# A linear-attention and Fourier-filter kernel: the transform split into even and odd bins, with a new instruction order

## The chip, the cores and the metric

One core of one Trainium2 chip. The metric is device time in microseconds of one execution; less is better. Engines: PE (TensorE, products; PEld its weight loads), DVE (VectorE), ACT (ScalarE), POOL (GpSimd, here only DMA issue and index tables), SP (SyncE, here only DMA issue).

## The reference

Shapes: q, k, v [8, 8, 576, 64], omega [128, 64], w_proj [512, 1536], filter_fft [576, 512], w_out [512, 512], all float32; the output is [8, 576, 512] float32.

```python
def phi(x):                                   # x: q or k, scaled by 64 ** -0.25
    proj = np.einsum('bhsd,md->bhsm', x, omega)
    h = proj - np.sum(x * x, axis=-1, keepdims=True) / 2.0
    h = h - np.max(h, axis=-1, keepdims=True)
    return np.exp(h) / np.sqrt(m)
kv = np.einsum('bhsm,bhsd->bhmd', k_p, v)
num = np.einsum('bhsm,bhmd->bhsd', q_p, kv)
den = np.einsum('bhsm,bhm->bhs', q_p, np.sum(k_p, axis=2))[..., None] + 1e-06
x = (num / den)                               # heads side by side: [8, 576, 512]
...
x1, x2, x3 = np.split(x @ w_proj, 3, axis=-1)
x2_conv = np.fft.irfft(np.fft.rfft(x2, n=S, axis=1) * np.fft.rfft(filter_fft, n=S, axis=0)[None], n=S, axis=1)
out = (x1 * x2_conv * x3) @ w_out
```

## The kernel before

**Two stages per batch.** `attention()` makes the rows of x, transposed to [512 columns, rows], in `xt`; `hyena()` does the projections, the circular convolution along the 576 rows and the output product. Each batch has 512 main rows (four tiles of 128) and 64 left rows; the left rows of two batches (a pair i) share one tile of 128, so that a pair is finished together (`xtl`, "left out").

**The transform.** 576 = 3 x 192. Rows are read as three chunks of 192. `fold` subtracts the third chunk from the first two (slots 0 and 1 of `xf`, 128 rows of each chunk, main rows alone) and adds all three (slot 3); `fold_rest` does the same for the last 64 rows of each chunk, which need the left rows (slot 2, both chunks side by side, and `xfl`). `project2` multiplies each slot by the middle third of w_proj, so that folding comes before the projection; the result is `x2`, slots 0 to 3, and `x2l`. `forward` then makes four banks of 128 spectral rows per batch: m = 0, 1, 2 of three products each (tables `fwb`, slots 2, 0, 1), for the bins that are no multiple of 3, and m = 3 of two products (`fwa`, `fwar`), for bins that are; one more bank, `xr`, for both batches of the pair (`fwn`, `fwnr`). ACT copies each bank to SBUF: m = 0 and 1 into `xs`, whose two banks are real and imaginary parts of the same bins, m = 2 and 3 into `sp`, where real and imaginary parts are the two partition halves of one bank. For those, two DMAs on SP's queue make `sw`, the copy with the halves exchanged. `spectrum` multiplies by the filter's spectrum on DVE: `ha`, `hb` for `xs`, `hps`, `hqs` for `sp` and `sw`. The inverse takes two column blocks at a time (g): three banks `pa`, even and odd of four products of 192 or 193 columns each, then ACT copies and DVE additions into `y`, and a multiplication by the gates `x13` (x1 times x3) gives `yt`. The output product with `wout` follows, per tile of 128 rows, an ACT copy and a DMA on SP.

**Tables and filter at the start.** `make_residues` scales index tables on ACT and reduces them on DVE; `sines` makes the sine and cosine tables `gtab`, `gta`, `gns` on ACT; `tables` turns them by PE transposes into `fwb`, `fwa`, `fwar`, `fwn`, `fwnr`. The filter is loaded in seven DMAs (`load_filter`), folded on DVE, transformed by the same tables, and moved into `hps` and `hqs` by DMAs on SP, as `split_out` has it: two ACT copies and four or five DMAs for a bank.

**The order.** Every operation is recorded by `Plan` and numbered; consecutive products into one bank are one number. `ORDER` is a list of these numbers, written out by hand or by a program beforehand, and `issue` emits them in that order (line 230, so that nearly all instructions of the profile have this line). Each engine runs its own instructions in this order, and a tile's buffer is given to the next tile of the same name when its last reader is done. PSUM has four banks named `h` and two double banks named `a`.

Lines of note: `turn_runs` (738 to 750) turns x for batches 0 and 1 by products with the identity into a float32 bank. `xs`, `sp`, `sw` and `bt` have two buffers each; `y` uses `bt` too. The last output tile, batch 7 tile 3, is copied half by DVE and half by ACT from one bank (1340 to 1354).

Of the kernel before, what the change touches and what calls it, by code (L numbers as in the profile page):

```python
# [26 lines left out]
599 29 33 31 34 56 30 9 0 32 57 3 5 4 38 27 39 28 6 2 40 35 50 49 7 51 52 45 46 55 53 11 12 23 47 41  # L27
42 43 71 99 24 48 72 138 8 85 97 44 70 1 26 54 74 73 16 18 13 86 25 87 10 88 37 76 586 64 98 588 589
36 65 100 67 69 58 66 68 600 89 59 90 91 590 75 60 62 61 143 149 92 63 140 93 112 114 150 152 154
155 587 145 14 22 21 111 591 113 151 153 161 101 108 110 156 94 102 107 109 103 104 105 157 163 162  # L30
159 95 106 164 139 158 160 165 96 115 116 126 127 211 120 181 121 128 182 123 229 122 124 125 117 20
144 172 223 118 119 174 175 177 166 230 167 176 135 178 133 593 224 171 247 134 136 131 129 225 173
130 132 227 596 168 169 170 17 19 214 595 603 602 604 179 180 615 617 248 195 196 197 616 146 618
192 193 194 147 231 233 15 78 611 613 249 213 189 217 623 597 250 592 598 190 186 191 625 594 187
188 258 260 624 83 221 286 626 200 201 202 204 203 137 183 185 184 226 321 612 198 205 206 609 199
734 614 228 207 601 661 322 208 610 232 673 662 262 660 81 212 235 236 80 289 670 736 209 290 234
632 251 264 735 257 605 210 259 148 215 77 218 606 674 671 252 667 216 672 237 291 295 668 296 238
293 675 607 292 253 261 347 627 142 737 254 350 676 628 141 255 669 256 294 679 680 284 222 738 687
663 82 348 220 79 263 298 297 740 664 608 665 299 688 629 300 726 677 678 728 239 240 241 242 244
630 243 245 246 265 266 631 666 305 685 686 641 642 643 267 275 633 648 649 650 689 647 652 655 651  # L40
645 276 277 693 694 705 278 691 692 706 634 636 635 656 657 707 653 708 644 709 637 279 306 280 281
282 654 639 646 268 269 307 308 309 270 681 658 659 323 682 310 283 324 365 325 271 366 272 219 303
739 359 304 367 369 371 372 360 319 301 320 741 695 362 342 619 273 690 727 302 700 696 343 697 364
621 373 344 274 823 361 822 729 374 722 723 363 316 724 480 311 620 730 699 701 318 474 725 313 745
315 312 732 747 710 684 683 349 622 345 638 640 702 698 703 746 375 731 749 748 317 314 704 346 713
714 758 326 355 329 742 733 330 743 353 288 287 351 331 760 893 840 895 368 385 370 824 744 386 829
841 711 712 337 451 452 327 376 377 378 328 720 338 750 842 751 719 752 334 335 379 830 285 332 383
384 333 425 476 354 897 848 899 849 356 357 894 755 339 336 394 756 432 757 477 358 434 340 715 896
753 825 387 721 754 905 716 341 832 844 845 388 717 826 827 907 419 481 396 828 428 781 782 783 759
898 900 718 430 762 393 862 833 389 863 856 857 771 917 761 773 390 395 919 831 391 768 769 784 838  # L50
770 839 786 772 427 397 84 843 774 763 775 764 765 767 776 766 381 846 399 847 429 785 834 835 777
778 852 853 431 398 433 836 850 837 851 400 392 380 483 352 787 382 800 801 401 402 788 435 789 790
794 403 404 906 405 908 486 882 411 436 876 489 412 795 877 858 859 491 802 437 438 413 791 780 921
878 879 860 855 864 865 861 406 493 922 803 495 779 439 854 881 407 793 408 440 883 804 414 415 866
416 818 918 488 479 424 923 819 490 475 924 453 454 417 920 870 867 869 871 455 418 874 884 909 911
426 880 891 890 449 820 805 409 821 796 872 450 446 410 469 797 496 448 798 925 868 497 873 470 471
927 885 792 926 928 932 886 892 441 498 443 934 499 887 472 799 910 912 806 888 945 423 422 875 807
947 492 473 442 444 1027 500 501 502 1092 901 903 1094 946 445 485 889 1009 447 902 948 949 904 503
1093 958 494 462 960 959 463 1095 459 942 943 482 961 944 929 930 1014 962 460 950 951 952 464 1015
537 808 1084 1086 931 815 933 465 816 809 810 811 817 1080 1082 505 954 953 466 467 935 484 420 421  # L60
478 936 461 1081 456 457 1012 1013 955 971 973 956 458 507 937 1083 938 468 543 544 957 963 939 545
1010 1011 940 1035 546 1036 913 812 1085 563 915 564 1087 540 539 972 914 984 1028 941 542 813 508
916 1029 1019 487 985 986 541 975 974 1031 509 1020 1032 1051 1104 1106 504 968 1018 510 511 512 513
964 519 521 1052 514 1016 1017 1033 516 969 970 1100 1102 1034 1021 515 518 1105 1101 517 1045 965
506 976 1030 520 1022 1046 522 523 1103 547 1023 548 549 1107 550 524 1025 530 977 978 525 979 980
526 538 1026 1096 1043 1044 1047 1098 1097 1037 1038 1024 1048 527 1049 1088 1090 1050 1099 528 529
531 533 1039 534 967 1005 1006 1112 535 814 1114 532 536 557 554 559 966 996 999 556 1000 1040 551
1053 1089 553 555 558 997 1065 560 1066 1054 1055 1057 1091 1056 1279 565 1113 566 1058 552 1059
1115 998 1042 1001 1041 1215 1061 561 1071 567 562 1069 574 575 576 1070 1063 577 578 1064 1068 1281
981 982 983 1072 990 1132 579 991 992 581 582 1271 1273 583 1060 1197 1280 571 584 1062 1282 1134  # L70
993 572 573 1275 994 585 1120 1277 1116 1117 1118 568 1119 1276 1121 1214 1196 1199 569 1007 1008
995 1272 1067 570 1278 1200 1133 1123 1222 1122 1274 1135 1124 1198 1125 1136 1002 1223 1201 580
1129 1203 1202 1003 1130 1204 1004 1131 1230 1108 987 1231 988 989 1126 1218 1205 1127 1206 1216
1219 1220 1221 1236 1237 1238 1232 1233 1110 1235 1234 1137 1128 1208 1239 1209 1078 1077 1079 1138
1073 1217 1224 1225 1139 1140 1074 1174 1175 1176 1076 1155 1159 1157 1075 1158 1160 1210 1211 1156
1171 1177 1178 1179 1207 1240 1241 1141 1162 1161 1163 1164 1244 1165 1109 1111 1167 1166 1172 1245
1246 1173 1145 1147 1212 1213 1287 1289 1226 1142 1227 1143 1144 1146 1250 1251 1149 1242 1148 1243
1150 1267 1306 1308 1269 1268 1151 1152 1270 1154 1288 1252 1253 1258 1228 1229 1290 1255 1254 1259
1256 1257 1168 1247 1153 1169 1170 1248 1260 1261 1249 1319 1186 1307 1187 1188 1299 1321 1301 1310
1263 1265 1309 1264 1303 1304 1305 1311 1295 1316 1192 1297 1266 1193 1194 1195 1300 1318 1262 1302  # L80
1320 1323 1322 1312 1313 1315 1317 1324 1325 1326 1283 1285 1296 1345 1332 1334 1347 1284 1342 1286
1344 1343 1298 1180 1346 1329 1181 1182 1333 1291 1331 1330 1293 1327 1314 1328 1348 1349 1361 1362
1350 1363 1336 1335 1351 1337 1338 1339 1364 1355 1365 1356 1357 1366 1189 1183 1292 1352 1184 1185
1190 1191 1341 1354 1340 1294 1353 1358 1359 1360 1367 1368 1370 1369 1371 1372 1373 1377 1378 1379
1380 1374 1381 1383 1382 1384 1375 1376
# [148 lines left out]
def kernel(  # L234
# [24 lines left out]
    EC = CH + 1  # L259
# [64 lines left out]
    fi = nc.tile(const, [P, 4], FP32, name="fi")  # L324
    fp = nc.tile(const, [P, 1], FP32, name="fp")
    si = nc.tile(hy, [P, 1024], FP32, name="x2", bufs=2)

    def first_constants():
        was, nc.where = nc.where, ("start", 0)
        iota = partial(nc.gpsimd.iota, allow_small_or_imprecise_dtypes=True)  # L330
        iota(fi[:, 0:1], pattern=[[1, 1]], base=1, channel_multiplier=3)
        for r in (slice(0, 64), slice(64, 128)):
            iota(fi[r, 1:3], pattern=[[-385, 2]], base=385, channel_multiplier=3)
        iota(si[:, 0 : 2 * CH], pattern=[[1, 2 * CH]], base=0, channel_multiplier=0)
        iota(fp[:], pattern=[[0, 1]], base=0, channel_multiplier=1)
        nc.vector.tensor_scalar(
            out=ident[:], in0=si[:, 0:P], scalar1=fp[:, 0:1], scalar2=None, op0=ALU.is_equal
        )
        nc.where = was
# [49 lines left out]

    fwb = nc.tile(const, [P, 9, P], BF16, name="fwb")
    fwa = nc.tile(const, [P, P], BF16, name="fwa")
    fwar = nc.tile(const, [P, 2, P], BF16, name="fwar")
    fwn = nc.tile(const, [P, 2, P], BF16, name="fwn")
    fwnr = nc.tile(const, [P, P], BF16, name="fwnr")
    gtab = nc.tile(const, [P, 3, 2 * CH], BF16, name="gtab")  # L400
    gta = nc.tile(const, [P, HC + P], BF16, name="gta")
# [997 lines left out]
```

## Time and profile before

| | |
|---|---|
| median of 3 runs | 258.19 us (257.41 to 259.14) |
| the profiled execution | 259.44 us |
| its span, first to last instruction | 257.4 us, mean granted clock of TensorE 0.997 |
| `out_dram<-osb`, 256 KB, SP | 24 issues, median 2.3 us to landing |
| `sw<-sp`, 128 KB, SP | 16 issues, median 2.4 us to landing |

Groups of instructions that the change touches, from the view that keeps shapes apart:

| engine, operation | count | busy us | mean ns |
|---|---|---|---|
| PE h<-x,fwb 128x512 | 72 | 18.6 | 379 |
| PE h<-yt,fwb 128x512 (filter) | 9 | 2.4 | 379 |
| DVE xf<-xt 128x1024 | 8 | 5.4 | 674 |
| DVE xf<-xt,xtl 128x512 | 8 | 3.2 | 403 |
| DVE bt<-xs,hb and xs<-xs,ha 128x1024 | 8 and 8 | 5.4 and 5.5 | 670 and 686 |
| DVE xs<-xs,bt 128x512 | 16 | 6.6 | 418 |
| DVE sp<-sp,hps, sw<-sw,hqs, sp<-sp,sw 128x1024 | 8 each | 5.5 each | 682 to 686 |
| DVE bt<-bt,osb 128x768 fp16 | 16 | 8.7 | 545 |
| DVE xb<-bt 128x384 fp16 | 16 | 5.7 | 354 |
| DVE vc<-vn,vc 128x2048 bf16 | 8 | 9.7 | 1218 |
| ACT xt<-h 128x512 from float32 (batches 0, 1) | 8 | 4.5 | 612 |
| ACT xt<-h 128x1024 from bf16 | 6 | 6.2 | 1032 |
| ACT gtab, 128x384 sines | 3 | 1.7 | 599 to 614 |

Busy time is the time in which an engine's records cover; records of one engine overlap a little. The record of a product spans from its start to its modelled end, so that starts show the pace better than durations. Idle time has behind it what released the engine.

### The profile page before, as it was taken

How to read it: one execution, taken by the hardware profiler on the slowest of the kernel's cores; microseconds unless marked ns; L12 is line 12 of the kernel's file. 1: busy time of each engine (PE TensorE's matmuls, PEld its weight loads, DVE VectorE, ACT ScalarE, POOL GpSimd, SP SyncE). 2: the span in 40 equal slices, each digit the busy share in tenths (PEclk: the TensorE clock that was granted, in tenths of full speed). 3: DMA queues.
4: the chain of work that ended last, by engine and by line, in shares of the span. 5: the costliest groups of instructions: out<-in, count | busy, mean ns of one | idle time of the engine just before them, and what ended most of it. 6: DMA issues, size and time to landing. Idle time of an engine off the chain costs nothing.

```text
span 257.4 us, 5843 instructions
## 1 busy us (share of the span) xinstructions
PE 238.1 (92%) x2282; PEld 139.2 (54%) x2282; DVE 217.9 (85%) x494; ACT 200.7 (78%) x324; POOL 62.6 (24%) x87
## 2 busy tenths in 40 slices
PE   0688699999999999999999979999999999999993
PEld 0555565655667465545566635555555545556641
DVE  6879998589697989999999887999867899899970
ACT  4689398899999999996888847894786568757653
POOL 8456363784007209403037000000000000000000
PEclk9999999999999999999999999999999999999998
DMA  6999999999938999998999977431635524223166
GB/s 83 184 193 178 198 173 140 146 167 176 155 85 128 157 141 110 160 138 142 149 230 128 177 91 188 100 68 34 140 110 143 109 80 122 81 62 113 52 230 220
DMA packets 86787, 35.28 MB, mean 137 GB/s; under 512 B 58219, under 2 KB 81256, under 8 KB 86760
## 3 DMA queue, kind: packets, MB, share of 16 engines
q0 software_dynamic: 59616, 17.31, 65.0%
q1 hardware_dynamic: 27000, 17.47, 27.4%
q8 instruction: 18, 0.29, 0.5%
q10 hardware_dynamic: 144, 0.13, 0.2%
q14 instruction: 9, 0.07, 0.1%
HBM read 34.64 MB, written 9.44 MB: 171 GB/s over the span
## 4 chain that ended last, share of the span: by engine, by line
PE 71%; DVE 10%; DMA 9%; ACT 6%; issue 1%; POOL 1%; SPq 0%; ACTq 0%; DVEq 0%
PE h L230 59%; PE a L230 12%; DMA qn<-in_q_dram 4%; DMA out_dram<-osb 4%; ACT osb L230 2%; DMA sw<-sp 1%; DVE h L230 1%; DVE vc L230 1%; DVE xb L230 1%; DVE kt L230 1%; ACT x L230 1%; DVE xt L230 1%; DVE vcl L230 1%; DVE qt L230 1%; ACT yt L230 1%
## 5 line engine op out<-in xcount | busy, mean ns | idle before, releaser
L230 PE MATMUL h<-xt,wproj 128*128 128x512 bf16 x256 | 64.5, 379 | 1.6 <-ACT osb L230 1.6
L230 ACT CAST x<-h 128x512 bf16<-128x512 f32 x68 | 40.1, 606 | 13.3 <-PE h L230 12.9
L230 PEld LDWEIGHTS <-wproj 128*128 128x128 bf16 x384 | 31.1, 98 | 27.5 <-issue 3.7
L230 ACT ACTIVATE osb<-h 128x512 f32<-128x512 f32 (+4 forms) x49 | 27.2, 566 | 12.5 <-PE h L230 4.1
L230 ACT ACTIVATE eqt<-a 128x1024 bf16<-128x1024 f32 x32 | 32.6, 1048 | 3.4 <-PE a L230 3.1
L230 ACT ACTIVATE ek<-a 128x1024 bf16<-128x1024 f32 x32 | 33.1, 1050 | 1.7 <-PE a L230 1.6
L230 PE MATMUL h<-wproj,xf 128*128 128x512 bf16 x128 | 32.4, 379 | 0.0
L230 PE MATMUL h<-wout,yt 128*128 128x512 bf16 x128 | 31.4, 379 | 0.0
L230 POOL DMA_DIRECT2D qn<-in_q_dram x26 | 23.7, 918 | 20.3 <-DMA qt<-qn 12.6
L230 DVE TENSOR_TENSOR x<-h,x 128x512 bf16<-128x512 f32 x32 | 21.7, 685 | 5.2 <-PE h L230 4.3
L230 PEld LDWEIGHTS <-yt 128*128 128x128 bf16 x128 | 12.1, 98 | 13.8 <-DVE vc L230 0.4
L230 PEld LDWEIGHTS <-xf 128*128 128x128 bf16 x134 | 12.1, 98 | 12.7 <-issue 1.0
L230 PE MATMUL h<-x,fwb 128*128 128x512 bf16 x72 | 18.6, 379 | 0.0
L230 DVE TENSOR_TENSOR xb<-a,rden 128x512 bf16<-128x512 f32 x24 | 16.2, 684 | 0.4
L230 PEld LDWEIGHTS <-eqt 128*128 128x128 bf16 x256 | 11.7, 98 | 6.0 <-DVE xb L230 1.0
L230 PE MATMUL a<-om,kt 64*128 64x128 bf16 x256 | 13.2, 231 | 1.3 <-ACT eqt L230 0.5
L230 PE MATMUL a<-kv,eqt 128*128 128x65 bf16 x256 | 13.0, 194 | 1.5 <-DVE xb L230 0.8
L230 PE MATMUL h<-ident,qn 128*128 128x128 bf16 x80 | 7.2, 238 | 7.4 <-DMA qn<-in_q_dram 7.4
L230 ACT CAST sp<-h 128x512 bf16<-128x512 f32 x16 | 9.7, 603 | 5.6 <-PE h L230 5.5
L230 DVE RECIPROCAL rden<-a 128x8 f32<-128x8 f32 x36 | 7.1, 200 | 7.1 <-PE a L230 6.9
L230 PE MATMUL h<-gtab,xs 128*128 128x193 bf16 x64 | 13.0, 247 | 0.0
L230 PE MATMUL a<-qt,om 64*128 64x512 bf16 x64 | 11.6, 389 | 1.1 <-ACT ek L230 0.3
(164 smaller groups left out, 512.1 us busy)
## 6 DMA issues: line engine op xcount, KB each, us to landing
out_dram<-osb SPq DMA_DIRECT2D x24, 256.0 KB, 2.3
vn<-in_v_dram POOLq DMA_DIRECT2D x8, 512.0 KB, 8.3
kn<-in_k_dram POOLq DMA_DIRECT2D x7, 512.0 KB, 8.6
qn<-in_q_dram POOLq DMA_DIRECT2D x24, 128.0 KB, 8.2
sw<-sp SPq DMA_DIRECT2D x16, 128.0 KB, 2.4
wproj<-in_moe_w_proj_dram POOLq DMA_DIRECT2D x3, 512.0 KB, 8.2
qn<-in_q_dram POOLq DMA_DIRECT2D x2, 512.0 KB, 7.6
out_dram<-xf SPq DMA_DIRECT2D x4, 256.0 KB, 2.9
```

The costliest lines, as they stand in the source:

```text
L230: getattr(real, name)(*args, **kw)
```

## The change

1. *Even and odd bins.* The rows are read as six blocks of 96. Differences d (blocks 0 and 4, less block 2) and w (blocks 3 and 1, less block 5) are made for all 96 rows, and slots 0 and 1 of `xf` are d + w and d - w of the first 64 rows, slot 2 the same of the other 32. Block 5 takes in the left rows. So only slot 3 is folded and projected from the main rows alone. The four banks of `forward` now all have real and imaginary parts as halves: m = 0 has two products, m = 1 two, m = 2 three, m = 3 two.
2. *Spectrum.* All four banks lie in `sp`; one exchange of all of it follows the last copy; three DVE operations of 2048 elements do the multiplication. `ha`, `hb`, `xs` and `bt` of the spectrum go.
3. *Inverse.* Products of 192 columns throughout, and another grouping of the additions, one more per g.
4. *Buffers.* d and w together, `sp` and the exchanged copy are all named `sp`, with three buffers.
5. *Start.* Three sine operations for five, index tables of 192 columns made from small constants; the dummy activation that was Sin is Exp. The filter comes in two loads; after folding on 96 partitions ten DMAs on SP place its rows; five banks go through `split_out`, three before.
6. *Outputs turned as bf16.* `turn_runs` uses PE transposes into a bf16 bank, two column blocks at a time.
7. *Last output tile* in 384 and 128 columns, each with its own bank, copied by ACT and DVE.
8. *A new ORDER*, of 1438 operations (1385 before). It ends, on PE, with batch 7's left rows, tile 2, the two parts of tile 3, tile 0, tile 1.

```diff
@@ start
-        nc.scalar.activation(out=sn[:], in_=zb[:], func=AF.Sin)
+        nc.scalar.activation(out=sn[:], in_=zb[:], func=AF.Exp)
...
+        for n, lo, hi in ((0, 4.0, 4.0 - 384.0), (1, 1.0, 1.0 - 384.0), (3, 0.0, -192.0)):
+            nc.vector.memset(cs[lo64, n : n + 1], lo)
+            nc.vector.memset(cs[hi64, n : n + 1], hi)
...
+        sine(ph[:, 0:1], gtab[:], r[:, 0:3])
+        sine(ph[:, 1:2], gta[:], r[:, 3])
+        sine(ph[:, 0:1], gn[:], r[:, 4])
@@ filter
-        nc.gpsimd.dma_start(out=ff[:, 0:3], in_=fsrc[0:P])
...
+        fsrc = moe_filter_fft.rearrange("(b x r) n -> x r b n", b=3, x=2)
+        for x in range(2):
+            f_ = nc.tile(hy, [P, 4, DM], BF16, name="yt", bufs=2)
+            nc.gpsimd.dma_start(out=f_[0:HC, 0:3], in_=fsrc[x])
...
+        for j in range(2):
+            move(out=fd[SL * j : SL * j + SL, 0:2], in_=fh[0:SL, 2 * j : 2 * j + 2])
+            for x in range(2):
+                q0 = 64 * x + 32 * j
+                move(out=fd[q0 : q0 + 32, 2], in_=fh[SL:HC, 2 * j + x])
+            move(out=fl[SL * j : SL * j + SL], in_=fb[32:HC, 3])
+        move(out=fd[0:HC, 3], in_=fa[:, 3])
+        move(out=fd[HC:P, 3], in_=fb[0:32, 3])
+    TERMS = (((0, 0), (1, 2)), ((2, 1), (3, 2)), ((4, 0), (5, 1), (6, 2)))
-        for z in (hqs[:, 1, :], fwar[:], vcl_buf[1][:]):
+        for z in (hqs[:, 3, :], fwar[:], fwb[:], gz[:], vcl_buf[1][:]):
             nc.vector.memset(z, 0.0)
@@ turn_runs
-            nc.tensor.matmul(
-                out=ps[:].rearrange("p (x t) -> p t x", t=NT)[:, t],
...
+        for u in range(2):
+            for t in range(NT):
+                nc.tensor.transpose(out=pb[:, u, t], in_=xbs[t][:, c + u], identity=ident[:])
+        nc.scalar.copy(
+            out=xt[:, c : c + 2, 0:SM].rearrange("p c (x t) -> p c t x", t=NT), in_=pb
+        )
@@ fold, fold_rest
-            nc.vector.tensor_tensor(
-                out=xf[:, 0:2],
...
+            dw = nc.tile(hy, [P, 2, CB, 2, HC], BF16, name="sp", bufs=3)
+            d_, w_ = dw[:, 0], dw[:, 1]
+            tt = nc.vector.tensor_tensor
+            tt(out=d_, in0=blocks[:, :, 0::4], in1=pair(blocks[:, :, 2]), op=ALU.subtract)
+            odd = blocks[:, :, 3::-2]
+            tt(out=w_[:, :, :, 0:32], in0=odd[:, :, :, 0:32], in1=pair(xt[:, :, 5 * HC : SM]), op=ALU.subtract)
+            tt(out=w_[:, :, :, 32:HC], in0=odd[:, :, :, 32:HC], in1=pair(xr), op=ALU.subtract)
+            for x, op in ((0, ALU.add), (1, ALU.subtract)):
+                tt(
+                    out=xf[:, x].rearrange("p c (j r) -> p c j r", j=2),
...
+                tt(
+                    out=xf[:, 2, :, SL * x : SL * x + SL].rearrange("p c (j r) -> p c j r", j=2),
...
@@ projections
-                for sl in (0, 1, 3):
-                    project2(x2[:, sl, :], xf[:, sl])
+                project2(x2[:, 3, :], xf[:, 3])
...
-                project2(x2s[bb][:, 2, :], xfs[bb][:, 2])
+                for sl in range(3):
+                    project2(x2s[bb][:, sl, :], xfs[bb][:, sl])
@@ forward, spectrum
+                sp = nc.tile(hy, [P, 4, DM], BF16, name="sp", bufs=3)
+                for m in (3, 2, 0, 1):
                     pf = bank()
...
+                    nc.scalar.copy(out=sp[:, m, :], in_=pf[:])
+                sw = nc.tile(hy, [P, 4, DM], BF16, name="sp", bufs=3)
+                nc.sync.dma_start(out=sw[lo64], in_=sp[hi64])
+                nc.sync.dma_start(out=sw[hi64], in_=sp[lo64])
+                spectrum(sp, sw)
...
+            nc.vector.tensor_tensor(out=sp[:], in0=sp[:], in1=hps[:, 0:4], op=ALU.mult)
+            nc.vector.tensor_tensor(out=sw[:], in0=sw[:], in1=hqs[:, 0:4], op=ALU.mult)
             nc.vector.tensor_tensor(out=sp[:], in0=sp[:], in1=sw[:], op=ALU.add)
@@ inverse
-                    nc.vector.tensor_tensor(
-                        out=yw,
-                        in0=yw,
-                        in1=ya[:, 0].unsqueeze(2).to_broadcast([P, 2, 2, CH]),
...
+                    for h, at in ((0, y[:, :, 0::4]), (1, y[:, :, 1:4:2])):
+                        tt(
+                            out=at,
+                            in0=at,
+                            in1=yv[:, :, h].unsqueeze(2).to_broadcast([P, 2, 2, HC]),
...
@@ out
+                        for k_, cs in enumerate((slice(0, 384), slice(384, DM))):
...
+                            (nc.scalar, nc.sync)[k_].dma_start(
+                                out=out[b, t * P : (t + 1) * P, cs], in_=osb
+                            )
```

## The prediction

> **What bounds the kernel now.** I began with the busy times and their forty slices.
>
> ```profile
> PE 238.1 (92%) x2282; PEld 139.2 (54%) x2282; DVE 217.9 (85%) x494; ACT 200.7 (78%) x324; POOL 62.6 (24%) x87
> PE   0688699999999999999999979999999999999993
> DVE  6879998589697989999999887999867899899970
> ```
>
> TensorE is full from slice 7 (38 us) on, with one dip near 150 us. Then the same by stretches: PE, weight loads, DVE, ACT, POOL, each with its instructions.
>
> ```profile
> 38.00:50.00 12.00, 11.90 (x146) 7.78 (x142) 8.34 (x22) 10.49 (x16) 6.66 (x9) 1.00 1.27 141
> 94.00:120.00 26.00, 26.00 (x246) 14.96 (x247) 24.50 (x55) 25.39 (x42) 10.68 (x14) 1.00 1.20 137
> 120.00:150.00 30.00, 30.00 (x314) 17.79 (x313) 28.27 (x63) 24.37 (x40) 7.36 (x9) 1.00 1.28 167
> 180.00:205.00 25.00, 24.95 (x239) 14.23 (x238) 18.90 (x40) 17.74 (x32) 0.00 (x0) 1.00 0.49 124
> ```
>
> The second engine is VectorE: 94% busy from 94 to 150 us, 76% from 180 to 205. Over 38 to 245 us all such stretches leave it 26 us idle. That PE is bound by its own work and not kept waiting, the waits of PE after 38 us say; this is their whole list:
>
> ```profile
> PE h L230 <- ACT osb L230: 1.6, 1, 1.6
> PE h L230 <- DMA qn<-in_q_dram: 0.2, 1, 0.2
> ```
>
> So there are three parts: a start of 38 us in which PE is idle for 13.3 us (13.0+12.0+13.0 less 4.47+10.40+9.88), 215 us of PE work, and an end. The end, from the timeline:
>
> ```profile
> 249.76 3.62 PE L230 MATMUL h<-wout,yt 128*128 128x512 bf16 x16
> 252.56 0.42 DVE L230 TENSOR_SCALAR osb<-h 128x256 f32<-128x256 f32 x1 [2.83 <-PE h L230]
> 253.01 0.39 ACT L230 ACTIVATE osb<-h 128x256 f32<-128x256 f32 x1 [0.72 <-DVE osb L230]
> 253.43 0.37 ACTq L230 DMA_DIRECT2D out_dram<-osb  x1
> 253.84 0.60 ACT L230 ACTIVATE x<-h 128x512 f32<-128x512 f32 x1 [0.45 <-ACT osb L230]
> 254.47 0.33 SPq L230 DMA_DIRECT2D out_dram<-x  x1
> ```
>
> Sixteen products of 512 columns take 3.62 us, of which the last one's record is 0.379: (3.62-0.379)/15 = 0.216 us each. That spacing, not the recorded 379 ns, is the price of one.
>
> **The change, part by part.** The products and calls of the changed program are counted from the diff, in the order in which it records them. The sum is against the profiled execution's 259.44 us (span 257.4), 1.25 above the median 258.19; I move the result by the same difference.
>
> *Forward products.* Per batch 9 products on fwb become 7, the two of m=3 stay: 16 fewer in all, 16 x 0.216 = 3.46 us. The filter's own transform loses 2: 0.43. Inverse products stay 12 for each pair of column blocks; 193 columns become 192, nothing. Turning outputs for batches 0 and 1 stays 32 products of 128 columns. Since nothing but PE's own work ends the waits there, I take the full -3.9. The Trainium skill, TensorE: Matmul & The Clock Gate, Back-to-back issue gap, gives 131 ns as the sustained spacing at 512 columns; the trace shows 216, and by the page the 18 products would be worth only 2.4 us. I go by the trace.
>
> *VectorE work.* By rows of before, bf16 additions: 256 elements 0.28, 512 0.42, 1024 0.68, 2048 1.21; 768 of fp16 0.55. Per batch:
> fold loses its 1024-element subtraction, -0.67. The rest's fold loses one of 0.40 and gains d (768, 0.55), w (256 and 512, 0.28+0.42) and two times (512 and 256): 0.55+0.70+1.40-0.40 = +2.25. The spectrum loses two multiplications (0.67+0.69) and two additions (2 x 0.42), and its other three grow from 1024 to 2048: 3 x (1.21-0.69) = 1.56, so -0.64. The inverse splits one addition of 768 (0.55) in two of 384 (0.355): +0.16, twice, +0.32. Together +1.26, for 8 batches +10 us. Set-up: the folded filter +1.8 (8 x 0.42 + 2 x 0.69 for 7 x 0.42), copies into tables +1.3, zeroing fwb, gz and small constants +1.2. In all +14 by durations and 48 instructions more; neighbours overlap by about 0.06 (the timeline starts one before the other's end), so some +11 of busy time: 218 becomes 229. These lie beside PE work, in the 26 us of idle time. Where the cover is gone (94 to 150 us, where 3.3 us are idle and some 3 are added) they make PE wait. Bounds: 0 if the new order spreads them, 6 us if half of the 11 can't be spread. I take +1.0, near the lower end, because at 94% of VectorE PE shows no wait.
>
> *The three class slots now wait for the left rows.* Before, 2 of 4 projections of a batch needed only its own 512 rows. What is queued behind them on PE: gates and attention of the next pair, ready earlier. In the new order, counted call by call, 21 groups of products stand between the last batch's forward and its first inverse product, where 13 stood. With 0.86 for four products of 512, 0.33 for four of 193 and 1.06 for sixteen of 128, that is 14 x 0.86 + 6 x 0.33 + 2 x 1.06 = 16.1 us for 6 x 0.86 + 5 x 0.33 + 2 x 1.06 = 8.9. So its longer chain is covered: copy 0.6, exchange, 3 x 1.21. Zero; uncovered it would be the rival below.
>
> *Exchange of halves (sw).* 16 transfers, 128 KB each at 2.4 us, become 256 KB; the outputs of 256 KB land in 2.3 to 2.9. So at most +0.5 each, with the issue after the fourth copy, not the second (1.2 us of ACT later). Behind the 16 us above and, earlier, attention. Zero.
>
> *SP's queue.* Filter: 10 moves of its folded rows and 8 more of its halves. On SP an issue costs about 0.6 us (four in 2.46), so 31 x 0.6 = 19 us for 13 x 0.6 = 8, nearly all before the first spectrum. Behind these on SP stand the first exchanges, the transposes of keys of batch 5, then outputs. In before the queue first issues them at 68 us though it is free from 1 us on; the new fold can start when the filter has landed (two loads, near 20 us, for seven). Zero, or +5 if not.
>
> *ACT.* Turning outputs: 8 copies of 0.61 become 4 of 1.03, -0.8. Two halves-outs for two scalings, +1.2. Even, and ACT has 20% idle.
>
> *The start.* Five sines become three: 2.74 (3 x 0.60 + 2 x 0.47) becomes about 1.65, the first key rows are loaded before the left ones; against this some fourteen small constants (0.1 us apart) stand before the first scaling, and the early Sin preload is gone. An exchange of tables shows here as
>
> ```profile
> 11.97 1.28 ACT L230 ACT_TABLE_LOAD   x1
> 13.27 1.02 ACT L230 ACTIVATE ekl<-a 128x1024 bf16<-128x1024 f32 x1
> ```
>
> 1.30 us from load to next activation. One more may come, on the path only if ACT isn't waiting for DVE then (it waits 2.06 and 1.12 us in before). The Trainium skill, ScalarE: Activation LUTs, What ACT_TABLE_LOAD costs, prices a switch at 2.66 us with a drain and so speaks against giving the preload up; the trace has 1.30 and no drain, and by the page the upper end would be 1.4 higher. Also: the next keys' left rows stand in POOL's queue ahead of queries 1 and values 0, waiting until PE has turned the first ones. Bounds -1.5 (sines and VectorE's shorter list) to +2.5 (a table load 1.3, and values later by 1.2). I take -0.3.
>
> *The end.* The split tile's halves share a bank and ran one after the other; ACT started 253.84 where its rhythm of 0.86 (249.97, 250.83, 251.69) gives 253.42. In the new order two full tiles follow the split one, so its ACT issue of 0.37 is hidden: -0.4.
>
> Sum: -3.9 + 1.0 - 0.3 - 0.4 = -3.6. So 255.8 for the profiled execution, and 254.6 on the median.
>
> **Rivals.**
> *VectorE becomes the bound.* For: 229 us of it, plus 6 idle in the first 38 us and 8 in the last 12.4, make 243, only some 10 below the new end; stretches at 94%. Against: PE's products wait for no DVE after 38 us, and its weight loads, which run ahead of them, for 2.1 us in all. PE's gain of 4.3 with 4 us of new waits: 258.0, within 1%.
> *The exchange and its ring come too late: slower.* dw, sp and sw, six tiles of a pair, share three buffers; two hold the spectra until the inverse is done, so one is left for the exchange and the next pair's folding. If a fold waits for a spectrum, PE wants projections. Price: a chain of exchange 3.70 (the row of sw on the critical chain), issue 0.46, and 3.6 of VectorE, 7.8 us, less the other PE work; it decides when that work, some 3 us between two stages early on, is shorter than the chain. Two pairs at some 4 us, less 4.3 gained, or once with SP's +5: 258.2 + 4 = 262. Against it: attention fills PE until 205 us.
> *The products saved are not on the path* (PE waits elsewhere for as long): then only the end's 0.4 stays, 257.8; I count it with the first rival.
>
> **How the numbers follow.** Forecast (PE bound, less work) 0.55; VectorE or no path 0.28; late exchange 0.17. About 1% (2.6 us) is what a measurement here can tell from none. Of the forecast 0.52 is below 255.6 and 0.03 above; of the first rival 0.02 below, 0.23 within, 0.03 above 260.8; of the last 0.03 within, 0.14 above. So faster 0.54, same 0.29, slower 0.17. Range: from -3.9 -1.5 -0.4 = -5.8, with no new wait (252.4), to the first rival with the late start on top, 258.0 + 2.5 = 260.5; the slower case is left out.
>
> **What would show it.** Right: 56 products on fwb by x2 for 72, PE's waits after 38 us still under 3 us, DVE near 229, the last full tile's copy right behind its product. Wrong: PE waiting for DVE (xf, sp, bt) or for sw, ACT with three table loads and the first exponential later than 13.3 us, PE filling later than 38 us.

## The result and the profile after

The changed kernel takes 268.24 us (median of 4 runs, 265.72 to 269.4) where the kernel before takes 257.8 us beside it (4 runs). The ratio is 1.037, with a 95% interval of 1.033 to 1.041: 3.7% slower. The forecast was 254.6 us, the range 252.4 to 260.5; the time lies outside it, on the side that the forecast thought least likely. Ratios, here and below, leave out single executions in a slower state, so they need not be the quotient of the medians given. The profiled execution took 268.09 us, its span is 265.9.

Busy times, PE's forty slices, and the clock granted to TensorE, from the page of after:

```profile
PE 236.1 (89%) x2265; PEld 136.8 (51%) x2265; DVE 225.9 (85%) x542; ACT 206.7 (78%) x322; POOL 59.5 (22%) x80
...
PE   0576749979999979999999999999999998999993
...
PEclk9999597997999999999999999999999999999999
```

The work is what the change says: VectorE went from 217.9 to 225.9 us, PE has 17 products fewer. But PE's slices 2 to 6 are thin, 9 and 15 dip, and in slices 5, 7 and 10 the clock falls, which before it did in none of the stretches ahead of the end. In stretches (PE, weight loads, DVE, ACT, POOL, each with its instructions; then the clock, DMA share, GB/s):

```profile
25.00:38.00 13.00, 9.04 (x127) 7.16 (x126) 11.56 (x25) 6.47 (x7) 7.50 (x10) 0.74 1.59 191
38.00:50.00 12.00, 9.98 (x131) 5.59 (x130) 8.79 (x28) 10.72 (x14) 5.84 (x7) 0.86 1.66 195
50.00:66.00 16.00, 13.52 (x136) 7.44 (x136) 12.57 (x33) 14.81 (x16) 5.58 (x7) 0.89 1.72 192
```

Before, PE was busy for 11.90 us of 38 to 50 and for all of 50 to 66, at a clock of 1.00. Now it idles 2.0 and 2.5 us there, and works at a lower clock for part of the rest. The list of PE's waits from 38 us on, which held 1.8 us in all before, now begins so:

```profile
PE h L233 <- ACT xt L233: 3.6, 2, 1.9
PE h L233 <- DVE sp L233: 2.3, 2, 1.9
PE a L233 <- ACT eqt L233: 1.0, 2, 0.5
PE h L233 <- DVE xf L233: 0.7, 1, 0.7
```

The largest is a wait for ACT, for the copies of the outputs turned as bf16. Two of these copies, and two groups of four products, in the timeline:

```profile
33.62 2.45 ACT L233 COPY xt<-h 128x1024 bf16<-128x1024 bf16 x1
...
37.71 2.45 ACT L233 COPY xt<-h 128x1024 bf16<-128x1024 bf16 x1
...
40.21 1.86 PE L233 MATMUL h<-xt,wproj 128*128 128x512 bf16 x4 [1.93 <-ACT xt L233]
...
46.14 1.02 PE L233 MATMUL h<-xt,wproj 128*128 128x512 bf16 x4
```

The prediction priced such a copy at 1.03 us; it takes 2.45. PE stands 1.93 us for it, and the four products behind it take 1.86 us where the same four take 1.02 at 46 us. Slices of 3 us show the granted clock at that time (PE busy, products, clock, DMA share, GB/s):

```profile
22.00:25.00 3.00, 1.16 (x15) 1.00 1.62 188
25.00:28.00 3.00, 1.93 (x43) 0.70 1.71 185
28.00:31.00 3.00, 2.14 (x33) 0.50 1.60 193
...
37.00:40.00 3.00, 0.77 (x10) 0.97 2.13 166
40.00:43.00 3.00, 2.79 (x8) 0.50 1.47 222
```

Both times a slice in which PE is busy for 0.8 to 1.2 us of 3 is followed by a clock that falls to one half. So in this execution the wait of 1.93 us is paid twice: once idle, and once more in the next products. How far that holds elsewhere is said in the last section.

### The profile page after: what moved, and what is told of

It is laid out like the page before. It is cut to its first block, busy times and chain, and to the rows that moved or that the text cites. A ratio compares the mean times of both kernels' runs of the same rounds, so it can differ in the third digit from the quotient of the medians.

```text
span 265.9 us, 5881 instructions
## 1 busy us (share of the span) xinstructions
PE 236.1 (89%) x2265; PEld 136.8 (51%) x2265; DVE 225.9 (85%) x542; ACT 206.7 (78%) x322; POOL 59.5 (22%) x80
## 4 chain that ended last, share of the span: by engine, by line
PE 57%; DMA 13%; DVE 12%; ACT 10%; issue 3%; SPq 2%; POOL 1%; DVEq 0%; ACTq 0%; POOLq 0%
PE h L233 48%; PE a L233 9%; DVE sp L233 4%; ACT xt L233 4%; DMA vn<-in_v_dram 3%; SPq L233 2%; DMA kn<-in_k_dram 2%; DMA out_dram<-osb 2%; DMA hqs<-osb 2%; DMA sp<-sp 2%; ACT eqt L233 1%; DVE xb L233 1%; ACT osb L233 1%; DVE x L233 1%; DVE bt L233 1%
## 5 line engine op out<-in xcount | busy, mean ns | idle before, releaser
L233 PE MATMUL h<-xt,wproj 128*128 128x512 bf16 x256 | 65.6, 390 | 4.4 <-ACT xt L233 3.6
L233 ACT ACTIVATE osb<-h 128x512 f32<-128x512 f32 (+4 forms) x53 | 30.0, 571 | 8.7 <-PE h L233 5.7
L233 PE MATMUL h<-wout,yt 128*128 128x512 bf16 (+2 forms) x132 | 31.4, 372 | 0.0
L233 ACT CAST sp<-h 128x512 bf16<-128x512 f32 x32 | 18.7, 603 | 3.4 <-PE h L233 3.3
L233 PEld LDWEIGHTS <-xf 128*128 128x128 bf16 x128 | 11.3, 98 | 13.0 <-DVE xf L233 1.2
L233 PEld LDWEIGHTS <-sp 128*128 128x128 bf16 x160 | 13.6, 98 | 6.5 <-DVE sp L233 3.0
L233 ACT COPY xt<-h 128x1024 bf16<-128x1024 bf16 x10 | 15.8, 1616 | 0.2 <-PE h L233 0.2
L233 PE MATMUL h<-x,fwb 128*128 128x512 bf16 x56 | 15.4, 380 | 0.0
L233 PE MATMUL h<-gtab,sp 128*128 128x192 bf16 x64 | 12.5, 246 | 2.3 <-DVE sp L233 2.3
L233 PEld LDWEIGHTS <-kt 64*128 64x128 bf16 x256 | 8.3, 95 | 10.1 <-issue 7.9
```

The source lines that it names most:

```text
L233: getattr(real, name)(*args, **kw)
```

## The experiments

All ratios are to the kernel before, run beside it on the same chip, with 95% intervals. The groups e1 to e4, e5 to e7, e8 to e10, e11 to e14, and e15 each ran on another chip; a difference between ratios of two groups takes for granted that the ratio is the same on both. Where microseconds are worked out of a ratio, it is times the 258.19 us of before. Changes in the order of the instructions are shown by name, since the order itself is a list of numbers.

### Is it the turning?

My theory: the copy costs by the stride with which it writes. It reads a bank in the order in which it lies and writes every fourth bf16 element of `xt`, 8 bytes apart. Rivals: the start, VectorE's added work, the exchange. Three kernels tell.

**e1**: after, with the turning of before.

```diff
-nc.tensor.transpose(out=pb[:, u, t], in_=xbs[t][:, c + u], ...)     # 2 column blocks to a bf16 bank
-nc.scalar.copy(out=xt[:, c : c + 2, 0:SM].rearrange("p c (x t) -> p c t x", t=NT), in_=pb)
+nc.tensor.matmul(out=ps[:].rearrange("p (x t) -> p t x", t=NT)[:, t], ...)   # 1 block to a float32 bank
+nc.scalar.copy(out=xt[:, c, 0:SM], in_=ps[:])
```

> The changed kernel with the turning of batches 0 and 1 put back (four float32 products and a copy of 512 columns for each of four blocks, two of each in the place of one in the order). Theory A, the strided bf16 copy: its four copies of 2.4 us (the trace of after) hold PE back at 36 to 40 us and at 55 to 59 us, and after each such pause PE runs at half its clock for some us; with copies of 0.6 us the time falls from 268.2 by 5 to 8 us, to 260 to 263, PE's waits for ACT xt vanish and the granted clock from 25 to 66 us rises from 0.74, 0.86, 0.89 to 0.95 or more. Rival B, the later chains (exchange, VectorE at 94%): only the copies' own excess on ACT goes, 4 x (2.4 - 1.2) = 4.8 us of ACT time beside other work, and the time falls by under 2, to 266 or more.

Measured: 261.52 us, ratio 1.013 (1.007 to 1.019). The eight copies take 0.63 us each, PE's wait for `xt` falls to 1.1 us, and from 38 to 245 us the clock is 1.00. Between 25 and 38 us, where 0.95 or more was expected too, it is 0.61.

**e2**: after, where the copy writes in order and takes the step on its read, from PSUM; nothing else differs.

```diff
-out=xt[:, c : c + 2, 0:SM].rearrange("p c (x t) -> p c t x", t=NT), in_=pb
+out=xt[:, c : c + 2, 0:SM].rearrange("p c (x t) -> p c x t", t=NT), in_=pb.rearrange("p c t x -> p c x t")
```

> The changed kernel with the same bf16 turning, but ACT's copy walks the bank with the stride and writes SBUF contiguously. Theory A, if the write's stride of 8 bytes is what costs: copies of about 1.03 us like the other ones of 1024 columns, and 260 to 263. If the order of reading costs as much, copies stay near 2.4 us and the time near 268.

Measured: 261.56 us, ratio 1.008 (1.004 to 1.013). The group of these copies, ten in all, of which six (later batches) have no stride, first in after and then in e2 (busy and mean ns of one; idle before):

```profile
L233 ACT COPY xt<-h 128x1024 bf16<-128x1024 bf16 x10 | 15.8, 1616 | 0.2 <-PE h L233 0.2
```

```profile
L233 ACT COPY xt<-h 128x1024 bf16<-128x1024 bf16 x10 | 10.2, 1036 | 0.2 <-PE h L233 0.2
```

With the same bytes and the same reordering, done by the read (steps of 128 elements) and not by the write (steps of 4), the four cost no more than the other six. The strided write alone cost (15.8 - 10.2)/4 = 1.4 us each.

**e3**: before, with the turning of after alone (the lines of e1, the other way round).

> The kernel before with only the changed turning (bf16 bank, two blocks a copy, strided write), its order kept with the pair at the place of the first of the two. Theory A: copies of 2.4 us, 4 x 2.4 = 9.6 us of ACT for 8 x 0.61 = 4.9, and 258 becomes 260 to 264 by waits of PE for ACT xt. Rival B: copies lie beside other work, within 1 us of 258.

Measured: 266.46 us, ratio 1.031 (1.025 to 1.038), with clocks of 0.86 and 0.79 in 38 to 50 and 50 to 66 us. This one part makes the old kernel 8 us slower, more than the 2 to 6 that were expected. The four copies take 9.8 us in all, where the eight that they replace took 4.5. PE's largest wait there is not for `xt` (0.9 us) but for an exponential that stands behind two of the copies, 4.70 us together, on ScalarE:

```profile
PE a L229 <- ACT eql L229: 3.5, 1, 3.5
```

From after to e2 the ratio falls by 0.029, some 7 us: most of the loss. The theory holds for the cost of the copy, and the rivals must explain what is left: e2 is still 2.2 us above before, where 3.6 below was forecast.

### Are the saved products worth what was said?

**e4**: before, with two products instead of three in classes 0 and 1 of each batch. Its output is another, since a third of these two sums is left out.

```diff
-for kt_ in (2, 0, 1):
+for kt_ in (2, 0, 1) if m == 2 else (2, m):
```

> The kernel before with two products in place of three for m = 0 and m = 1 (slot 1, or slot 0, left out of the sum, so 16 forward products fewer; the filter keeps its nine; the output is not the reference's). If PE is bound by its own work, as the prediction had it: 258.2 - 3.5 = 254.7. If the products saved are not on the path: 257.5 or more.

Measured: 254.83 us, ratio 0.985 (0.980 to 0.990), 3.9 us faster (2.7 to 5.1) for 16 x 0.216 = 3.5. In the kernel before, the saved products are on the path, at the price that was read from the trace. An estimate by the 131 ns that the prediction cites from the Trainium skill (TensorE: Matmul & The Clock Gate, Back-to-back issue gap) makes 16 x 0.131 = 2.1, which lies outside the interval.

### What else holds up e2: start or exchange?

e2's clock is 0.61 between 25 and 38 us. PE's timeline there, ahead of the drop:

```profile
23.88 0.19 PE L233 MATMUL a<-vcl,ekl 128*128 128x65 bf16 x1 [0.53 <-ACT ek L233]
25.80 0.38 PE L233 MATMUL a<-vc,ek 128*128 128x65 bf16 x4 [1.73 <-DVE vc L233]
```

`vc` is made from the values of batch 0, whose load POOL issues at 14.9 us, behind the load of `kl` for pair 1, which stands 5.2 us for PE; before, it is issued at 8.7.

**e5**: e2, with these loads ahead.

```diff
-POOL: k1, filter 0, kl1, q1, vl0, v0
+POOL: k1, q1, vl0, v0, filter 0, kl1
```

> The kernel with the strided read (ratio 1.008, 13 us below the stage's clock of before: 0.61 in 25 to 38 us), with the loads of q1, of the left values and of v0 issued ahead of the first filter load and of the load of kl1, as the kernel before issues them. Theory START (what is left of the loss, some 6 us, lies in the first 40 us: the values of batch 0 land late because their load stands behind kl1, which waits 5.3 us for TensorE; TensorE pauses and then runs at half clock for 6 to 10 us): the granted clock of 25 to 38 us comes back to 0.95 or more and the time falls by 3 to 5 us, to a ratio of about 0.99 to 0.997. Rival EXCHANGE (the loss lies in the late spectra): the time falls by less than 1 us, whatever the clock of that stage. Rival ORDER (TensorE pauses there for something else, the copies and VectorE's new work at the start): the values land earlier but the clock stays near 0.6.

Measured: 265.73 us, ratio 1.028 (1.018 to 1.038). None of the theories said slower. VectorE's timeline gives the reason (start, duration, and the idle time ahead with what ended it):

```profile
21.37 0.42 DVE L233 TENSOR_TENSOR yt<-yt 96x512 bf16<-96x512 bf16 x1 [5.00 <-DMA yt<-in_moe_filter_fft_dram]
```

The first addition on the filter stands ahead of `kt` in VectorE's order. Its load, now behind q1 and v0, lands late; PE waits 4.7 us for `kt`, and the clock is 0.50 from 21 to 33 us. The wait had only been moved to another load.

**e6**: e2 without the 16 exchange transfers, VectorE's work as long as with them. The output is another.

```diff
-nc.sync.dma_start(out=sw[lo64], in_=sp[hi64]); nc.sync.dma_start(out=sw[hi64], in_=sp[lo64])
-nc.vector.tensor_tensor(out=sw[:], in0=sw[:], in1=hqs[:, 0:4], op=ALU.mult)
+nc.vector.tensor_tensor(out=sw[:], in0=hps[:, 0:4], in1=hqs[:, 0:4], op=ALU.mult)
```

> The kernel with the strided read, without the 16 transfers that exchange the halves of the spectra; VectorE's second product reads a table in place of the exchanged spectrum, so its work is as long as before. Leaves out the exchange, so the output is another. Theory EXCHANGE (256 KB that leave behind the last copy of a batch, 4.1 us, come late for TensorE's inverse products): 4 to 6 us faster than the kernel with the strided read, ratio 0.985 to 0.995. Theory START: less than 1.5 us faster, ratio 1.002 to 1.008.

Measured: 256.19 us, ratio 0.990 (0.986 to 0.994), 4.8 us (by the ratios) below e2. PE's waits from 38 to 245 us in e2 (its largest) and then in e6 (all of them):

```profile
PE h L233 <- DVE sp L233: 2.2, 2, 1.9
```

```profile
PE a L232 <- DVE xb L232: 0.8, 2, 0.6
PE a L232 <- DMA kt<-kn: 0.6, 1, 0.6
```

**e7**: e6, with two of the three VectorE operations of each spectrum (a product and the addition) removed as well.

> As the kernel without exchange, and with one of the three VectorE products of each spectrum (16 operations fewer, some 20 us of VectorE). Leaves out the exchange and the second half of the filter product. It bounds all that VectorE and the exchange can cost behind 60 us. Theory START: within 2 us of the kernel without exchange. Theory VECTOR (VectorE's added 11 us are what TensorE waits for): 3 us or more below the kernel without exchange.

Measured: 255.98 us, ratio 0.989 (0.981 to 0.998). Taking 16 operations of 1.22 us from VectorE changes nothing that can be seen. With the exchange away, VectorE isn't the bound; with it, no run takes VectorE's work out. The order up to 38 us is the same in e2, e6 and e7, and yet the clock there isn't (25 to 38 us in e2, then in e7):

```profile
25.00:38.00 13.00, 10.36 (x127) 7.99 (x126) 11.05 (x23) 5.51 (x7) 7.69 (x10) 0.61 1.58 191
```

```profile
25.00:38.00 13.00, 9.40 (x137) 6.21 (x138) 12.63 (x26) 8.64 (x13) 7.05 (x9) 1.00 1.58 191
```

e6 has 0.74. So the 0.61 of e2 is that of one execution, and can't be put down to the order alone.

**e8**: e5, with VectorE's two additions behind `vc`.

```diff
-DVE: filter add, kt (b1), rec, kt (b1), max of b0, filter add, rec, vcl, vc
+DVE: kt (b1), rec, kt (b1), max of b0, rec, vcl, vc, filter add, filter add
```

> The kernel with the strided read and with q1, the left values and v0 loaded first, and with VectorE's two additions on the loaded filter moved behind the first vc (in the run with the loads first, the first of these additions waited 5.0 us for its load and held up kt, for which TensorE waited 4.7). Theory START: with neither wait TensorE's clock stays at 0.95 or more from 20 to 38 us and the time falls to a ratio of 0.99 to 1.0 (3 to 4 us below the kernel with the strided read). Rival: what is late next (the exponentials, the filter's own tables) takes it back, and the ratio stays at 1.005 or more.

Measured: 259.29 us, ratio 1.005 (1.002 to 1.008), and the clock of 25 to 38 us is 0.87 (1.00 in e12, with the same start). The mean clock of its ten executions is 0.993 to 0.998, of those of e2 0.976 to 0.998. By the ratios it is 1 us below e2, and the intervals overlap. The time itself is between what both theories said.

### How does the exchange cost?

Two theories: VectorE's products wait for it (4.1 us to landing, against 2.4 for half the size before), or its traffic and its place on SP's queue hold up others.

**e9**: e2, with each exchange in two parts of two banks, the first after two copies (in batches 1, 3, 4, 5 and 7).

```diff
+for ms in (first two banks copied, other two):
-    nc.sync.dma_start(out=sw[lo64], in_=sp[hi64])
+    nc.sync.dma_start(out=sw[lo64, ms], in_=sp[hi64, ms])
```

> The kernel with the strided read; each exchange goes in two parts of two banks, the first part as soon as two of the four banks are copied (in batches 1, 3, 4, 5 and 7; in the others both parts leave where the whole did). Without the exchange the kernel is 5.3 us faster. Theory LATENCY (the 4.1 us from the last copy to the landing of 256 KB, ahead of three VectorE products, are what the inverse products wait for): the landing behind the last copy comes 1 to 1.5 us sooner, and the time falls by 1 to 3 us, ratio 0.997 to 1.005. Rival QUEUE (the transfers cost by their number and by the room they take on the queues, next to loads and stores): 16 more issues make it no faster, ratio 1.007 or more.

Measured: 273.70 us, ratio 1.061 (1.054 to 1.069). The list of all engines' waits from 80 to 125 us, and SP's queue:

```profile
DVE xr L235 <- DMA hps<-osb: 7.1, 1, 7.1
...
PE h L235 <- DVE xr L235: 6.0, 1, 6.0
```

```profile
95.80 1.28 SPq L235 DMA_DIRECT2D sp<-sp  x2
97.13 0.60 SPq L235 DMA_DIRECT2D hps<-osb  x1
```

My edit put the first part of batch 1 ahead of the last filter move for the left rows. SP waits for copies until 95.8 us; the move, which e2 issues at 90.3 us, comes at 97.1, and VectorE's `xr` and PE behind it stand 7 and 6 us. That is some half of the 14 us by which e9 is slower than e2; the rest was not followed. This run shows that a place on SP's queue can cost that much, and says nothing of the theory.

**e10**: e8 and e9 together.

> Strided read, loads first with the additions late, and the exchange in two, together. If START and LATENCY hold, the gains add: 4 to 6 us below the kernel with the strided read, ratio 0.985 to 0.993, faster than the kernel before. If both fall, 1.005 or more.

Measured: 272.77 us, ratio 1.055 (1.050 to 1.061): the same fault, with the move at 99.3 us and PE standing 4.8 us for `xr`.

**e11**: e2, where the transfers carry part of `wproj`, have the same size and place, and nobody reads them; VectorE's three operations run in place on `sp`. The output is another.

```diff
-nc.sync.dma_start(out=sw[lo64], in_=sp[hi64])
+nc.sync.dma_start(out=sw[lo64], in_=wproj[hi64] (its first 2048 columns))
```

> The kernel with the strided read (ratio 1.008); the 16 exchange transfers stay, with the same bytes, tiles and place on SP's queue, but carry a part of wproj and nobody reads them; VectorE's three products of each spectrum run in place on the spectrum, as long as before. Leaves out the exchange, so the output is another. Theory LATENCY (what the exchange costs is that VectorE's products wait for it): as fast as without the exchange, ratio 0.987 to 0.995. Rival TRAFFIC (bytes and issues slow the loads, stores and filter moves): ratio 1.002 to 1.008.

Measured: 258.41 us, ratio 1.002 (0.998 to 1.006), between e2 (1.008) and e6 (0.990); its interval overlaps that of e2. By the ratios 1.7 us of the 4.8 go when nobody waits, and 3.2 only when the transfers go; by the medians it is 3.1 and 2.2. So both theories seem to hold in part; the shares aren't settled. These transfers don't wait for the copies of the spectrum either (the second exchange goes at 90.46 us, in e2 at 97.57), so they also hold up SP's queue less.

**e12**: e8, with two parts in batches 3, 5 and 7 alone and SP's order otherwise kept.

> The kernel with the strided read, loads first and additions late (ratio 1.005), with the exchange in two parts in batches 3, 5 and 7 alone, the first part as soon as two banks are copied and SP's order otherwise unchanged. LATENCY: 0.5 to 2 us less, ratio 0.997 to 1.003, if these batches are among those that TensorE waits for. TRAFFIC: the same or slower, 1.004 or more.

Measured: 257.70 us, ratio 1.000 (0.996 to 1.003), 1.2 us below e8, and the intervals overlap. Its SP queue near 80 us shows the other part of the cost:

```profile
76.29 0.59 SPq L235 DMA_DIRECT2D hqs<-osb  x1
79.00 1.10 SPq L235 DMA_DIRECT2D sp<-sp  x2
80.14 0.63 SPq L235 DMA_DIRECT2D hqs<-osb  x1
```

The first exchange stands until 79.00 us: by the chain of waits, for VectorE's folding, which has one of the three buffers of that name. Behind it stands the last filter move, `hqs`, whose source is copied by 66 us. It lands at 85.3, and PE stands 1.9 us. In e11 the same move is as late (81.83 us), in e6 it isn't.

**e15**: e12, with this one move ahead of the exchange.

```diff
-SP: exchange b0, exchange b0, move hqs
+SP: move hqs, exchange b0, exchange b0
```

> The kernel with the strided read, loads first, additions late and two parts in batches 3, 5 and 7 (ratio 1.000), with one filter move put ahead of the first exchange on SP's queue. Theory QUEUE HEAD: the move is issued by 77 us and lands by 83, TensorE's wait of 1.9 us at 80 to 90 us falls under 0.8, and the time falls by 1 to 1.8 us: ratio 0.992 to 0.997, below the kernel before. Rival: the exchange itself, landing at 83 to 84 us, is next, and less than 0.6 us is won: ratio 0.997 to 1.001.

```profile
76.10 1.23 SPq L235 DMA_DIRECT2D hqs<-osb  x2
78.86 1.10 SPq L235 DMA_DIRECT2D sp<-sp  x2
```

Measured: 257.56 us, ratio 0.9955 (0.9926 to 0.9983); PE's wait for the first spectrum falls from 1.9 to 1.1 us, less than was expected. The intervals of e12 and e15 overlap, so the gain of this one move isn't shown by the times. e15 is the one version with the full output that is faster than before, by 0.2 to 0.7%, and it is 4% faster than the change as it was made.

### Does the account close?

**e13**: e8 without the exchange. The output is another.

> Strided read, loads first with additions late, and no exchange (VectorE's work as long as before; leaves out the exchange, so the output is another). If turning, start and exchange are the whole of the missed 13 us, this comes to the forecast of 254.6 us: 253 to 255.5, ratio 0.98 to 0.988. If something else of the change costs time too, 256 or more.

Measured: 255.84 us, ratio 0.992 (0.989 to 0.995), the same as e6 within the intervals, and above the 0.988 that was expected at most. From e8 to e13 the exchange costs 3.2 us by the ratios, from e2 to e6 4.8. Turning and exchange account for nearly all; the start's order shows no gain once the exchange is away. The forecast, 0.986, stays 1.6 us below. The start is the candidate: in its first 38 us PE is idle for 13.2 us before, and for 15.5 in e13, 16.5 in e15. No run separates it.

**e14**: before, with e2's turning (strided read) alone.

> The kernel before, with only the turning changed: bf16, four copies of 128x1024 that read with a stride and write in order, for eight of 128x512. By ScalarE's busy time 4 x (2 x 0.61 - 1.03) = 0.8 us less, beside other work: ratio 0.995 to 1.001. Rival: the copies, twice as long, come later for the first products on them, as with the strided write: ratio 1.005 or more.

Measured: 257.46 us, ratio 1.000 (0.996 to 1.004). By itself, done rightly, the turning as bf16 is worth nothing that can be seen here: the 0.8 us of ScalarE's busy time don't show in the time. It differs from e3 (1.031) only in the side on which the copy steps, and that is worth 8 us.

The account, by the ratios:

| step | kernel | ratio | us against before |
|---|---|---|---|
| forecast | | 0.986 | -3.6 |
| after | after | 1.037 | +9.6 |
| the copy's stride on the read | e2 | 1.008 | +2.2 |
| and no exchange | e6 | 0.990 | -2.7 |
| e2, with start, two parts, filter move | e15 | 0.9955 | -1.2 |

In the two traces, the span of after is 8.5 us longer: PE is idle for 10.5 us more (3.8 in the first 38 us, 4.4 from 38 to 66, 1.6 from 66 to 245, 0.6 behind) and busy for 2.0 less, where 3.9 less work was forecast.

## Why the prediction was wrong

**The step that failed stands under ACT: "Turning outputs: 8 copies of 0.61 become 4 of 1.03, -0.8", and "Even, and ACT has 20% idle".** The 1.03 was the row of copies of the same shape, but without a stride in what they write. With it they take 2.45. And the cover was not looked at in its place: ACT's idle time is an average, while in 38 to 66 us PE's next products stand right behind these copies, or behind what follows them on ScalarE (e3). No bound was set above 1.03. It cost 7 to 8 us (e2, e3). In 38 to 66 us of after there are 4.4 us more of idle time, of which e2 keeps 1.6, and, by the clocks of 0.86 and 0.89, up to 12 x 0.14 + 16 x 0.11 = 3.4 us of slower work.

**Exchange of halves: "at most +0.5 each", "Behind the 16 us above and, earlier, attention. Zero."** Wrong by 4.8 us (e2 to e6) or 3.2 (e8 to e13). The transfers took 4.1 us and not 2.3 to 2.9; the bound had come from stores to memory, not from the row of `sw` itself. The rival **"The exchange and its ring come too late"** named the mechanism, a buffer shared by folding and exchange, but priced it at 8 us with 0.17 and had no clause for what stands behind the waiting transfer on SP, which e12 and e15 show.

**SP's queue: "Zero, or +5 if not."** The moves do start earlier than before, near 37 us and not 68 (e2). What costs is order: one late move, 1.9 us of PE.

**The products, -3.9:** e4 takes out 16 of the 18, priced at 3.5, and measures 3.9 (2.7 to 5.1), in the kernel before. The price holds.

**VectorE, +11 of busy time, +1.0 of time:** busy +8.0, and no time that e7 can see, which has no exchange. So far the first rival falls; the third falls for the kernel before (e4).

**The start, -0.3 (bounds -1.5 to +2.5).** Three table loads were seen and are 1.28 each, yet the first exponential starts at 12.85 us, 0.4 earlier than before. The other clause, "values later by 1.2" behind POOL's queue, came true as a wait: PE stands 1.2 us for `vc` in after, 1.7 in e2, 0.4 before. That this set off the lower clock of 25 to 38 us isn't shown, since e7 and e9, with the same order, kept 1.00. By PE's idle time in the first 38 us the change as it was made starts 3.8 us worse (17.1 against 13.2, 1.0 of it a wait for the slow copies), beyond the upper bound; e13, with the loads moved ahead, 2.3 worse (15.5).

**The end, -0.4:** no run separates it.

**Among the signs named as wrong**, "PE waiting for DVE (xf, sp, bt)" came, as did three table loads and PE filling later than 38 us; a wait for ACT's `xt`, the largest, was not on the list.

## What to carry to other kernels

The row that prices a copy must have the same access pattern on both sides, not only the same shape and type; where none has, bound the price by more than the contiguous row, and put a stride on the side where it is measured to be free. Before a step is costed at nothing because its engine has idle time, look for who waits for it in that stretch, and reckon that a wait of TensorE of 2 us among sparse products can cost more than 2. A load or transfer that is moved on a queue, or made to wait on one, must be followed by what stands behind it: in e5, e9 and e15 that decided the time, and twice against my own edit.

## What the runs showed of the hardware

**A strided bf16 write by ScalarE.** 1024 elements per partition take 2.45 us where the write steps 8 bytes, and 1.03 where it is in order, even if the read from PSUM then steps by 256 bytes. The Trainium skill, SBUF — State Buffer, Door 1: The DMA port swizzle, says that two accesses to each line of 16 bytes keep full bandwidth, so that bf16 may step by up to 8 elements, and that any access to PSUM that isn't contiguous slows matmuls, which these copies are not. These copies step by 4 elements in SBUF and are slowed; the read from PSUM isn't. The measurement decides.

**The clock falls without a long pause.** In after, PE was busy 0.77 us of 37 to 40, with no wait above 1.93, and worked at 0.50 from 40 to 43. The Trainium skill, TensorE: Matmul & The Clock Gate, What's actually happening, halves the clock after an idle window of about 3.4 us; by that the waits here would have cost nothing more. Another section of that page, A second HAM failure mode, tells of short idle gaps that make the clock swing, and these rows fit that. But the busy share of one slice doesn't decide it: e9 was busy 0.83 us of 88 to 91 and kept 1.00 there and in the next slice, while e1 was busy 1.89 us of 22 to 25 and fell to 0.56. Nor does the order of the instructions alone (e2 and e7 above). What decides it, no run here shows.
